# First MLP in token tiles of 512, 512, 512 and 768, the last one's gate and value as seven block products; weight sums over DRAM; q kv in float32

## The chip, the cores and the metric

One NeuronCore of a Trainium2 chip runs the whole program. The metric is the device time of one execution in microseconds (us). The engines are TensorE (PE for the matrix products, PEld for loading their stationary operand), VectorE (DVE), ScalarE (ACT), GpSimd (POOL) and SyncE (SP). SP only issues DMAs; POOL issues DMAs here and little else.

## The reference

Linear attention without a softmax, then two MLPs, all on float32 arrays:

```python
kv  = einsum('bhsd,bhse->bhde', k, v)            # batch 4, 8 heads, 576 tokens, head size 64
out = einsum('bhsd,bhde->bhse', q, kv)
x   = out / sqrt(mean(out*out, -1) + 1e-6) * g_norm   # as 2304 tokens x 512
y   = (1 / (1 + exp(-(x @ w_gate)))) * (x @ w_val) @ w_out    # 512 -> 1536 -> 512
h   = y @ w_in2                                        # 512 -> 2048
res = (maximum(h, 0) + log1p(exp(-abs(h)))) @ w_out2   # 2048 -> 512
```

## The kernel before

Nearly all products are made in three passes: an operand is split into a high part (rounded by ScalarE, `split_hi` L65) and a low remainder (`split_lo` L68, VectorE), and `mm3` (L60) adds high times high, high times low and low times high in PSUM. The instructions of each engine stand in the order in which the code is written (a manual schedule); nothing reorders them, and engines wait for each other by semaphores.

The **first MLP** runs over five token tiles (`TILES1`, L25) of 512, 512, 384, 384 and 512 tokens, and in each over the 12 blocks of 128 hidden columns. I call one block of one tile a unit; there are 60, numbered 0 to 59. A unit is 12 matmuls for the gate (`ffn1_mm`, PSUM tile `ps_g`), 12 for the value (`ps_v`), and 12 that bring the previous unit's gated product back to 512 columns (`ffn1_out` L517, tiles `yacc`), each of as many columns as the tile has tokens. ScalarE takes the sigmoid of the gate, VectorE multiplies it by the value (`gated` L506), and both split the result into the tile `ghl`.

The attention of tiles 2 to 4 is woven into the units of the tile before. It goes in pieces of at most 256 tokens: a transpose of q on VectorE and its split (`q_trans` L434), three passes with the block-diagonal kv of two heads (`po_mm` L441, tile `po`), the square and its split (`po_evac`), two matmuls with a 128x128 matrix that averages over a head (`ss_mm` L457, tile `ss`), a copy of `ss`, a root on ScalarE, and a reciprocal and scaling of 128 partitions on VectorE (`rms_scale` L477).

The **second MLP** runs over three tiles of 768 tokens and eight pairs of hidden blocks each. Its first product is made of 2x2 blocks with seven products in place of eight (`product` L674, PSUM tiles `ps_b` and `ps_c`); the sums of weight blocks that it needs are made beside the first MLP (`m_sums`), stored to DRAM by POOL's queue and loaded again by SP's. The work beside the units is placed by hand: `at_place` (L928) hangs a step on a place of a unit ("A", "B", "C" for matmuls, "a", "bg", "b", "end", "c", "late" for the others), `M_PLAN` (L1016) holds the places of the second MLP's weights, and the main loop (L1128) runs a unit and what hangs on it. The first pair of the second MLP is woven into units 57 to 59.

## Time and profile before

| | |
|---|---|
| time, median of 3 runs | 892.74 us (892.72 to 893.12) |
| the profiled execution's own time | 894.41 us |
| span of its profile | 892.6 us |
| PE, PEld, DVE, ACT busy | 880.7, 780.0, 604.4, 487.4 us |
| DMA traffic | 188.50 MB, 211 GB/s over the span |

Busy time of PE is a union of overlapping records: a matmul of 512 columns is recorded with some 390 ns, but the next one starts some 227 ns after it. So what a run of matmuls takes is read from the start of one group of a timeline to the start of the next, divided by the count, and not from the recorded durations.

### The profile page before, as it was taken

How to read it: one execution, taken by the hardware profiler on the slowest of the kernel's cores; microseconds unless marked ns; L12 is line 12 of the kernel's file. 1: busy time of each engine (PE TensorE's matmuls, PEld its weight loads, DVE VectorE, ACT ScalarE, POOL GpSimd, SP SyncE). 2: the span in 40 equal slices, each digit the busy share in tenths (PEclk: the TensorE clock that was granted, in tenths of full speed). 3: DMA queues.
4: the chain of work that ended last, by engine and by line, in shares of the span. 5: the costliest groups of instructions: out<-in, count | busy, mean ns of one | idle time of the engine just before them, and what ended most of it. 6: DMA issues, size and time to landing. Idle time of an engine off the chain costs nothing.

```text
span 892.6 us, 12252 instructions
## 1 busy us (share of the span) xinstructions
PE 880.7 (99%) x4701; PEld 780.0 (87%) x4701; DVE 604.4 (68%) x884; ACT 487.4 (55%) x778; POOL 72.9 (8%) x112
## 2 busy tenths in 40 slices
PE   7899999999999999999999999999999999999998
PEld 6687888888899999999888889899898989989896
DVE  4888775475856676675577266578776678766666
ACT  5778754544554454643544264556655456554554
...
PEclk9999999999999999999999999999999999999999
...
GB/s 301 283 349 269 190 163 186 283 203 184 236 189 172 99 291 207 175 165 133 303 308 332 141 221 236 203 174 142 236 249 233 225 206 174 140 306 189 188 95 71
DMA packets 89114, 188.50 MB, mean 211 GB/s; under 512 B 35936, under 2 KB 61792, under 8 KB 76768
## 3 DMA queue, kind: packets, MB, share of 16 engines
...
## 4 chain that ended last, share of the span: by engine, by line
PE 95%; DMA 2%; SPq 2%; issue 0%; DVE 0%; ACT 0%
PE oacc L62 22%; PE yacc L62 17%; PE ps_g L62 16%; PE ps_v L62 16%; PE ps_b L680 11%; PE ps_c L680 9%; DMA kv_raw<-in_v_dram 2%; SPq L117 1%; PE kv_ps L272 1%; PE po L62 1%; DMA kv_raw<-in_k_dram 1%; PE o_rows L346 1%; PE qt L334 0%; PE ss L462 0%; PE ss L461 0%; SPq L772 0%
## 5 line engine op out<-in xcount | busy, mean ns | idle before, releaser
L62 PE MATMUL oacc<-w_up,g 128*128 128x512 f32 x864 | 205.2, 391 | 0.0
L62 PEld LDWEIGHTS oacc<-w_up,g 128*128 128x128 f32 x864 | 161.5, 188 | 31.8
L62 PE MATMUL ps_g<-x,w 128*128 128x512 f32 (+1 forms) x720 | 161.2, 372 | 1.5 <-ACT x L396 0.9
L62 PE MATMUL ps_v<-x,w 128*128 128x512 f32 (+1 forms) x720 | 159.8, 370 | 1.3 <-ACT w L66 1.3
L62 PE MATMUL yacc<-ghl,w 128*128 128x512 f32 (+1 forms) x720 | 160.0, 370 | 0.0
L62 PEld LDWEIGHTS ps_g<-x,w 128*128 128x128 f32 x720 | 131.7, 189 | 19.7 <-DVE x L397 1.4
L62 PEld LDWEIGHTS ps_v<-x,w 128*128 128x128 f32 x720 | 129.6, 188 | 18.4 <-ACT w L66 1.7
L62 PEld LDWEIGHTS yacc<-ghl,w 128*128 128x128 f32 x720 | 129.8, 188 | 16.9 <-DVE w L69 0.4
L680 PE MATMUL ps_b<-y_c,w_in 128*128 128x384 f32 x576 | 116.2, 336 | 0.0
L680 PEld LDWEIGHTS ps_b<-y_c,w_in 128*128 128x128 f32 x576 | 102.0, 188 | 2.4 <-DVE y_c L69 0.3
L66 ACT CAST ghl<-sg 128x512 fp32r<-128x512 f32 (+1 forms) x60 | 34.6, 577 | 106.9 <-DVE sg L509 106.9
L680 PE MATMUL ps_c<-y_c,w_in 128*128 128x384 f32 x432 | 87.6, 337 | 0.0
L1078 DVE TENSOR_TENSOR c<-ps_c,c 128x384 f32<-128x384 f32 x72 | 40.1, 557 | 61.1 <-ACT c L1075 31.5
L1075 ACT COPY c<-ps_b 128x384 f32<-128x384 f32 x72 | 34.6, 480 | 81.7 <-PE ps_b L680 80.0
L680 PEld LDWEIGHTS ps_c<-y_c,w_in 128*128 128x128 f32 x432 | 77.0, 188 | 2.1
L503 ACT ACTIVATE sg<-ps_g 128x512 f32<-128x512 f32 (+1 forms) x60 | 33.3, 555 | 74.2 <-PE ps_g L62 72.3
L509 DVE TENSOR_TENSOR sg<-sg,ps_v 128x512 f32<-128x512 f32 (+1 forms) x60 | 37.9, 631 | 51.8 <-PE ps_v L62 50.3
L692 ACT ACTIVATE e<-c 128x768 f32<-128x768 f32 x46 | 39.0, 848 | 49.9 <-DVE c L1078 49.1
L66 ACT CAST g<-c 128x768 fp32r<-128x768 f32 (+1 forms) x50 | 40.6, 812 | 30.9 <-DVE c L717 28.2
L712 DVE SCALAR_TENSOR_TENSOR u<-u,ln 128x768 f32<-128x768 f32 x46 | 43.9, 954 | 12.1 <-ACT ln L704 12.1
L69 DVE TENSOR_TENSOR ghl<-sg,ghl 128x512 fp32r<-128x512 f32 (+1 forms) x60 | 38.1, 635 | 16.8 <-ACT ghl L66 16.5
L69 DVE TENSOR_TENSOR g<-c,g 128x768 fp32r<-128x768 f32 (+1 forms) x50 | 46.2, 923 | 4.5 <-ACT g L66 4.4
...
## 6 DMA issues: line engine op xcount, KB each, us to landing
w_in<-wi_dram SPq DMA_DIRECT2D x42, 1024.0 KB, 6.9
w<-wo_dram SPq DMA_DIRECT2D x24, 1024.0 KB, 5.8
w_up<-wu_dram SPq DMA_DIRECT2D x24, 1024.0 KB, 6.4
...
```

Of the source, the lines that this page charges most:

```text
L62: nc.tensor.matmul(out=ps, lhsT=lhs(a), rhs=rhs(b), start=start and n == 0, stop=stop and n == 2)
L66: nc.scalar.copy(out=hi, in_=src)
L69: nc.vector.tensor_tensor(out=lo, in0=src, in1=hi.bitcast(F32), op=ALU.subtract)
L117: nc.sync.dma_start(out=t, in_=unit(w, f))
L272: nc.tensor.matmul(out=ps[sl, sl], lhsT=lhs, rhs=rhs, start=r == 0, stop=r == R)
L503: nc.scalar.activation(out=sg, in_=chain.pop(("g", t, i)), func=ACTF.Sigmoid)
L509: nc.vector.tensor_tensor(out=sg, in0=sg, in1=chain.pop(("v", t, i)), op=ALU.mult)
L680: nc.tensor.matmul(out=ps, lhsT=w[:, a, kk * P:(kk + 1) * P], rhs=y[:, b, kk], start=first and kk == 0 and n == 0, stop=kk == 1 and n == 2 ...
L692: nc.scalar.activation(out=e, in_=h_t[p][:, f], func=ACTF.Abs)
L712: nc.vector.scalar_tensor_tensor(out=u, in0=u, scalar=1.0, in1=ln_t.pop((p, f)), op0=ALU.subtract, op1=ALU.subtract)
L1075: nc.scalar.copy(out=p_part(n), in_=p_t["b"])
L1078: nc.vector.tensor_tensor(out=h_t[p][:, f, HT * th:HT * (th + 1)], in0=p_t["c"], in1=p_part(n), op=ALU.add)
```

## The change

The first MLP gets four tiles of 512, 512, 512 and 768 tokens, so 48 units in place of 60. The first three run as before. The last one (`unit3`) makes gate and value together as one 2x2 block product: seven products of 6 matmuls of 384 columns (`prod3`) in place of 24 matmuls for each 384 tokens, and 12 matmuls of 512 and 12 of 256 columns for the way back (`out3`). Four of its seven weight operands are sums of blocks of the gate's and value's weights, made on VectorE (`s_whole`, `s_sums`, `s_sums2`), split, stored to DRAM and loaded again (`s_load`), at the places of `S_PLAN`. The seven combinations of x (`x_sub`, `x_comb`) are made before the tile starts. The attention's pieces become 192 tokens (one tile's first piece 128), q times kv is one float32 matmul, the head sums go to 8 rows in place of 128, and their root goes to all partitions over DRAM (`rms_store`, `rms_load`). The second MLP's weights are placed anew; its pair 0 and pair 1 now stand behind the last unit, with the last unit's `out3` between their products.

```diff
-TILES1 = ((0, 512), (512, 512), (1024, 384), (1408, 384), (1792, 512))
+TILES1 = ((0, 512), (512, 512), (1024, 512), (1536, 768))
 TM2, HT = 768, 384
-PIECE = 256
+PIECE = 192
+ORDER = (6, 7, 0, 8, 1, 9, 2, 10, 3, 11, 4, 5)
...
     def po_mm(u, piece, hp):
         b, s0, c0, m = piece
-        ps = atp.tile([P, PIECE], F32, tag="at", name="po")[:, :m]
+        if hp == 0:
+            ss_t[u, c0] = atp.tile([P, 512], F32, tag="at", name="ss")[:8, :m]
+            po_t[u, c0] = atp.tile([P, 512], F32, tag="at", name="po")[:, :m]
+        ps = po_t[u, c0]
         t = hl_t.pop(("q", u, c0, hp))
-        mm3(ps, lambda a: kvb[:, a, hp], lambda b: t[:, b, :m], True, True)
+        nc.tensor.matmul(out=ps, lhsT=kvp[:, (b + 1) % 2, hp], rhs=t, start=True, stop=True)
         at_ps["po", u, c0, hp] = ps
...
     def po_evac(u, piece, hp):
...
         ps = at_ps.pop(("po", u, c0, hp))
         sq = scr.tile([P, PIECE], F32, tag="s", name="sq")[:, :m]
         nc.scalar.activation(out=sq, in_=ps, func=ACTF.Square)
-        nc.vector.tensor_copy(out=of_tile(u)[:, hp, c0:c0 + m], in_=ps)
+        nc.scalar.copy(out=of_rows(u, hp)[:, c0:c0 + m], in_=ps)
         hl_t["s", u, c0, hp] = t = hlpool.tile([P, 2, PIECE], F32R, tag="hl", name="hl")
         split(t[:, HI, :m], t[:, LO, :m], sq)
...
     def ss_mm(u, piece, hp):
         b, s0, c0, m = piece
-        ps = atp.tile([P, PIECE], F32, tag="at", name="ss")[:, :m]
-        t = hl_t.pop(("s", u, c0, hp))
-        nc.tensor.matmul(out=ps, lhsT=ones, rhs=t[:, HI, :m], start=True, stop=False)
-        nc.tensor.matmul(out=ps, lhsT=ones, rhs=t[:, LO, :m], start=False, stop=True)
-        at_ps["ss", u, c0, hp] = ps
-
-    def ss_evac(u, piece, hp):
-        b, s0, c0, m = piece
-        ps = at_ps.pop(("ss", u, c0, hp))
-        if hp == 0:
-            ms_t[u, c0] = stage.tile([P, NP, PIECE], F32, tag="st", name="ms")
-        nc.scalar.copy(out=ms_t[u, c0][:, hp, :m], in_=ps)
+        ps, t = ss_t[u, c0], hl_t.pop(("s", u, c0, hp))
+        for a in (HI, LO):
+            nc.tensor.matmul(out=ps, lhsT=ones[:, hp], rhs=t[:, a, :m], start=hp == 0 and a == HI,
+                             stop=hp == NP - 1 and a == LO, skip_group_check=True)
 
     def rms_root(u, piece):
         b, s0, c0, m = piece
-        ms = ms_t[u, c0][:, :, :m]
-        nc.scalar.activation(out=ms, in_=ms, func=ACTF.Sqrt, bias=eps)
-
-    def rms_scale(u, piece, hps):
+        r = rpool.tile([8, PIECE], F32, tag="r", name="r")[:, :m]
+        nc.scalar.activation(out=r, in_=ss_t[u, c0], func=ACTF.Sqrt, bias=eps[:8])
+        r_t[u, c0] = r
+
+    def rms_store(u, piece):
         b, s0, c0, m = piece
-        ms = ms_t[u, c0][:, hps, :m]
-        of = of_t[u][:, hps, c0:c0 + m]
-        nc.vector.reciprocal(out=ms, in_=ms)
+        nc.vector.reciprocal(out=r_t[u, c0], in_=r_t[u, c0])
+        t0 = TILES1[u][0] + c0
+        nc.sync.dma_start(out=r_dram[:, t0:t0 + m], in_=r_t.pop((u, c0)))
+
...
+    def s_whole(f):
+        s_f[f] = t = block("c1", [P, 8, 256], F32, "s_f")
+        w = W["gv", f]
+        nc.vector.tensor_tensor(out=t[:, :4].rearrange("p (j c) m -> p j (c m)", j=2), in0=w[:, :, HI].bitcast(F32),
+                                in1=w[:, :, LO].bitcast(F32), op=ALU.add)
...
+    def s_sums2(f):
+        w11, w12, w21, w22, s2, s1, s3, s4 = (s_f[f][:, n] for n in range(8))
+        nc.vector.tensor_tensor(out=s2, in0=s1, in1=w11, op=ALU.subtract)
+        nc.vector.tensor_tensor(out=s4, in0=w12, in1=s2, op=ALU.subtract)
+
+    def s_round(f):
+        y = block("c2", [P, 8, 256], F32R, "s_y")
+        s_y[f] = y[:, :4], y[:, 4:]
+        split_hi(s_y[f][HI], s_f[f][:, 4:])
+        if f != ORDER[0]:
+            nc.gpsimd.dma_start(out=ws_dram[f][:, :, HI], in_=s_y[f][HI].bitcast(F32))
+
...
+    def prod3(f, ps, name, comb, first):
+        lhs, x = lhs3(f, name), x_c[comb]
+        for k in range(2):
+            for n, (a, b) in enumerate(PASSES):
+                nc.tensor.matmul(out=ps, lhsT=lhs(a, k), rhs=x[:, b, k],
+                                 start=first and k == 0 and n == 0, stop=k == 1 and n == 2, skip_group_check=True)
+
+    yacc3 = []
...
+        for h in range(2):
+            for m in ms:
+                for n, (a, b) in enumerate(PASSES):
+                    nc.tensor.matmul(out=yacc3[m][h], lhsT=w[:, a, m * P:(m + 1) * P],
+                                     rhs=g[:, b, 512 * h:512 + 256 * h], start=i == 0 and n == 0 and (h == 0 or m % 2 == 0),
+                                     stop=i == F1 - 1 and n == 2, skip_group_check=True)
...
+    def unit3(i, run):
+        f = ORDER[i]
+        pb, pc = (mm.tile([P, TM1], F32, tag="mm", name="ps_" + n)[:, :HT] for n in "gv")
+        p0, p1, p2_, t0, t1, t2 = left
+        add = lambda out, part: nc.vector.tensor_tensor(out=out, in0=pc, in1=part, op=ALU.add)
+        copy, act, mult = nc.scalar.copy, nc.scalar.activation, ALU.mult
+        gap_a, gap_b = gap3(i)
+        prod3(f, pb, "11", "11", True)
+        copy(out=p0, in_=pb)
+        prod3(f, pc, "12", "21", True)
+        add(t0, p0)
+        run("a")
+        prod3(f, pb, "S2", "T2", False)
+        copy(out=p1, in_=pb)
+        act(out=t0, in_=t0, func=ACTF.Sigmoid)
+        run("bg")
+        prod3(f, pc, "S1", "T1", True)
+        prod3(f, pb, "S3", "T3", False)
+        copy(out=p2_, in_=pb)
+        add(t2, p2_)
+        gap_a()
+        run("b")
+        prod3(f, pc, "S4", "22", False)
+        add(t1, p1)
+        prod3(f, pb, "22", "T4", False)
+        act(out=t1, in_=t1, func=ACTF.Sigmoid)
+        g = gl[i]
+        for h, t in ((0, t0), (1, t1)):
+            nc.vector.tensor_tensor(out=t, in0=t, in1=t2 if h else pb, op=mult)
+            split_hi(g[:, HI, HT * h:HT * (h + 1)], t)
+        for h, t in ((0, t0), (1, t1)):
+            split_lo(g[:, LO, HT * h:HT * (h + 1)], t, g[:, HI, HT * h:HT * (h + 1)])
+        run("end")
+        if gap_b:
+            gap_b()
+        run("late")
+
+    Y_HOME = ("b8", "b10", "b11", "b0", "b1", "b2", "b3", "b4", "b5")
     y_raw, y_c, n_y, n_lo = {}, {}, [0], [0]
...
-    M_PLAN = ((30, 35, 36, 40, 40, 50, 50, 54, 56, 61, 62),
...
+    M_PLAN = ((32, 33, 33, 34, 34, 37, 39, 39, 41, 37, 41, 43, 44, 44, 52, 52),
...
+    S_PLAN = ((0, (60, 60, 61, 62, 62)),
+              (1, (63, 65, 65, 65, 66)),
+              (2, (68, 68, 68, 70, 70)),
...
+    y_split("T1")
+    p_open()
+    while n_fed[0] < 5:
+        feed_next()
...
+    s_u(0, 0)
+    s_max(0, 0)
+    out3(last, (1,))
+    p_close()
+    p_start(1)
+    p_11(1)
+    p_copy(0)
+    s_ln(0, 0)
+    s_exp(0, 1)
+    p_12(1)
+    p_add(1, 0, 0, 0)
+    s_u2(0, 0)
+    s_sub(0, 0)
+    s_u(0, 1)
+    y_out3(0)
+    p_s2(1)
+    p_copy(1)
+    s_hi(0, 0)
+    s_max(0, 1)
...
```

How the order of instructions moves, in three places. First TensorE, two units of the 384-token tile 3 before (`po` and `ss` are the attention of the next tile):

```order
L62 MATMUL ps_v<-x,w 128x384 x12
L62 MATMUL po<-hl,kvb 128x256 x3
L62 MATMUL yacc<-ghl,w 128x384 x12
L62 MATMUL ps_g<-x,w 128x384 x12
L461 MATMUL ss<-hl,ones 128x256
L462 MATMUL ss<-hl,ones 128x256
L62 MATMUL ps_v<-x,w 128x384 x12
L62 MATMUL po<-hl,kvb 128x256 x3
L62 MATMUL yacc<-ghl,w 128x384 x12
```

and one unit of the last tile after (`ps_g` and `ps_v` are the two banks of the block products, `x_c` the combinations of x, `s_in` weight sums and `w` or `w_k` weights from DRAM, `yacc` the way back of the unit before):

```order
L668 MATMUL ps_g<-x_c,w_k 128x384 x6
L668 MATMUL ps_v<-x_c,w_k 128x384 x6
L668 MATMUL ps_g<-x_c,s_in 128x384 x6
L668 MATMUL ps_v<-x_c,s_in 128x384 x6
L668 MATMUL ps_g<-x_c,s_in 128x384 x6
L683 MATMUL yacc<-ghl,w 128x512 x6
L683 MATMUL yacc<-ghl,w 128x256 x6
L668 MATMUL ps_v<-x_c,s_in 128x384 x6
L668 MATMUL ps_g<-x_c,w_k 128x384 x6
L683 MATMUL yacc<-ghl,w 128x512 x6
L683 MATMUL yacc<-ghl,w 128x256 x6
```

Three groups of 12 matmuls a unit have become seven of 6 with two groups of 12 between and behind them. Second VectorE, from the last `sg` of one tile into the next; before, from tile 3 into tile 4 (`sg` the gated product, `ghl` its low part, `ys` the copy of `yacc`, `m_raw` and `m_f` second-MLP weights):

```order
L509 TENSOR_TENSOR sg<-sg,ps_v 128x384
L69 TENSOR_TENSOR ghl<-sg,ghl 128x384
L509 TENSOR_TENSOR sg<-sg,ps_v 128x512
L69 TENSOR_TENSOR ghl<-sg,ghl 128x512
L538 COPY ys<-yacc 128x384 x2
L610 SCALAR_TENSOR_TENSOR m_raw<-m_raw 128x1024
L613 SCALAR_TENSOR_TENSOR m_f<-m_raw 128x1024
L509 TENSOR_TENSOR sg<-sg,ps_v 128x512
```

and after, from tile 2 into the last tile (`s_y` the low part of weight sums, `x_c` that of x combinations, `t` the sums and the gated product of `unit3`):

```order
L545 TENSOR_TENSOR sg<-sg,ps_v 128x512
L70 TENSOR_TENSOR s_y<-s_f,s_y 128x1024
L70 TENSOR_TENSOR x_c<-of,x_c 128x768
L70 TENSOR_TENSOR ghl<-sg,ghl 128x512
L70 TENSOR_TENSOR x_c<-of,x_c 128x768 x2
L702 TENSOR_TENSOR t<-ps_v,t 128x384 x2
L576 COPY ys<-yacc 128x512 x2
L798 SCALAR_TENSOR_TENSOR m_raw<-m_raw 128x1024
L702 TENSOR_TENSOR t<-ps_v,t 128x384
L726 TENSOR_TENSOR t<-t,ps_g 128x384
L726 TENSOR_TENSOR t<-t 128x384
L70 TENSOR_TENSOR ghl<-t,ghl 128x384 x2
```

The unit's own additions out of PSUM (`t<-ps_v`) now stand behind the low parts of three combinations of x, of a weight sum and of `ghl`, and one of them behind `ys` and `m_raw`. Third ScalarE in the pair that follows the first MLP; before, from the end of pair 0 into pair 1 (`c<-ps_b` copies a partial sum out of PSUM, `g` is a high part, `e` and `ln` are the softplus of pair 0):

```order
L1081 COPY c<-ps_b 128x384
L692 ACTIVATE e<-c 128x768
L696 ACTIVATE e<-e 128x768
L66 CAST g_4755<-c 128x768
L1075 COPY c<-ps_b 128x384
L704 ACTIVATE ln<-u 128x768
L536 COPY ys<-yacc 128x512
L1075 COPY c<-ps_b 128x384
L536 COPY ys<-yacc 128x512
L1075 COPY c<-ps_b 128x384
```

and after, at the same place:

```order
L890 ACTIVATE e<-e 128x768
L1309 COPY c<-ps_b 128x384
L886 ACTIVATE e<-c 128x768
L1303 COPY c<-ps_b 128x384
L898 ACTIVATE ln<-u 128x768
L890 ACTIVATE e<-e 128x768
L689 COPY ys<-yacc 128x512
L1303 COPY c<-ps_b 128x384
L67 CAST g_4652<-c 128x768
L898 ACTIVATE ln<-u 128x768
L1303 COPY c<-ps_b 128x384
```

The first `c<-ps_b` in either is pair 0's last. Between it and pair 1's first copy stood `abs`, `exp` and `g`, and now `abs` alone; between pair 1's first and second copy stood `ln` and one `ys` copy, and now `ln`, `exp` and `ys`; its third copy now stands behind `g` and `ln` of pair 0.

## Rows read from the trace of the kernel before

**Rows 1.** Page, part 1: busy us (share of the span) xinstructions of the engines.

```profile
PE 880.7 (99%) x4701; PEld 780.0 (87%) x4701; DVE 604.4 (68%) x884; ACT 487.4 (55%) x778; POOL 72.9 (8%) x112
```

**Rows 2.** Page, part 2: busy tenths in 40 slices, and the granted clock.

```profile
PE   7899999999999999999999999999999999999998
DVE  4888775475856676675577266578776678766666
PEclk9999999999999999999999999999999999999999
```

**Rows 3.** Waits of PE: line, releaser: us in total, times, longest; first and last of six.

```profile
PE kv_ps L272 <- DMA kv_raw<-in_v_dram: 2.6, 3, 1.8
...
PE kv_ps L272 <- DMA kv_raw<-in_k_dram: 0.4, 1, 0.4
```

**Rows 4.** Timeline, PE, 384-token tile: start us, us, engine line op out<-in xcount.

```profile
386.16 0.52 PE L62 MATMUL po<-hl,kvb 128*128 128x256 f32 x3
386.51 2.27 PE L62 MATMUL yacc<-ghl,w 128*128 128x384 f32 x12
388.62 2.24 PE L62 MATMUL ps_g<-x,w 128*128 128x384 f32 x12
390.70 0.28 PE L461 MATMUL ss<-hl,ones 128*128 128x256 f32 x1
390.82 0.28 PE L462 MATMUL ss<-hl,ones 128*128 128x256 f32 x1
390.94 2.25 PE L62 MATMUL ps_v<-x,w 128*128 128x384 f32 x12
```

**Rows 5.** Timeline, PE, a 512-token tile.

```profile
235.64 2.88 PE L62 MATMUL yacc<-ghl,w 128*128 128x512 f32 x12
238.36 2.88 PE L62 MATMUL ps_g<-x,w 128*128 128x512 f32 x12
```

**Rows 6.** Timeline, PE, float32 matmuls of 128 columns (two records each).

```profile
57.81 1.05 PE L334 MATMUL qt<-kvf,kv_raw 128*128 128x128 f32 x8
58.62 2.98 PE L62 MATMUL ps_v<-x,w 128*128 128x512 f32 x12
```

**Rows 7.** Timeline, PE, matmuls of 64 columns.

```profile
304.47 0.75 PE L62 MATMUL po<-hl,kvb 128*128 128x64 f32 x6
305.06 2.33 PE L62 MATMUL yacc<-ghl,w 128*128 128x384 f32 x12
```

**Rows 8.** Timeline, PE, block products of the second MLP.

```profile
601.52 1.20 PE L680 MATMUL ps_b<-y_c,w_in 128*128 128x384 f32 x6
602.57 1.23 PE L680 MATMUL ps_c<-y_c,w_in 128*128 128x384 f32 x6
```

**Rows 9.** Lines by form, DVE: names, shapes xcount | busy us, mean ns | idle before.

```profile
L509 DVE TENSOR_TENSOR sg<-sg,ps_v 128x512 f32<-128x512 f32 x36 | 24.6, 684 | 41.7 <-PE ps_v L62 40.4 <-ACT m_raw L129 1.0
L1078 DVE TENSOR_TENSOR c<-ps_c,c 128x384 f32<-128x384 f32 x72 | 40.1, 557 | 61.1 <-ACT c L1075 31.5 <-PE ps_c L680 28.9 <-issue 0.4
L613 DVE SCALAR_TENSOR_TENSOR m_f<-m_raw 128x1024 uint32<-128x1024 uint32 x16 | 19.6, 1226 | 2.5 <-DMA wi_dram<-m_f 2.0
L623 DVE TENSOR_TENSOR m_f<-m_f 128x256 f32<-128x256 f32 x8 | 3.4, 425 | 0.3
L481 DVE RECIPROCAL ms<-ms 128x256 f32<-128x256 f32 x12 | 20.9, 1746 | 0.0
```

**Rows 10.** Lines by form, ACT.

```profile
L704 ACT ACTIVATE ln<-u 128x768 f32<-128x768 f32 x46 | 38.7, 841 | 0.1
L1075 ACT COPY c<-ps_b 128x384 f32<-128x384 f32 x72 | 34.6, 480 | 81.7 <-PE ps_b L680 80.0 <-issue 1.7
L503 ACT ACT_TABLE_LOAD x8 | 10.3, 1283 | 1.2 <-PE ps_g L62 1.1
L536 ACT COPY ys<-yacc 128x512 f32<-128x512 f32 x6 | 3.3, 582 | 0.0
```

**Rows 11.** DMA issues: names, queue, xcount, KB each, median us to landing.

```profile
w<-wo_dram SPq DMA_DIRECT2D x24, 1024.0 KB, 5.8
```

More of the change, by code (lines that the diff above doesn't have):

```diff
@@ new lines, in prod3, with out3 @@
+    def prod3(f, ps, name, comb, first):
[5 more added lines that the diff above has]
+    yacc3 = []
+    def out3(i, ms):
+        f, g = ORDER[i], gl[i]
+        w = W["o", LAST, f]
+        if i == 0 and not yacc3:
+            full = [acc.tile([P, 512], F32, tag="acc", name="yacc") for _ in range(KD)]
+            half = [atp.tile([P, 2, 256], F32, tag="at", name="yacc") for _ in range(2)]
+            yacc3.extend((full[m], half[m // 2][:, m % 2]) for m in range(KD))
+        for h in range(2):
[4 more added lines that the diff above has]
+                                     stop=i == F1 - 1 and n == 2, skip_group_check=True)
@@ L1129, in attention_moe_moe_kernel @@
         prev = its[n - 1]
+        q_prev = prev[1] * (F1 // 2) + prev[2] // 2
+        if t == LAST:
+            unit3(i, lambda place: run(n, place))
+            if i % 2 == 0 and q_prev + 2 < NT1 * F1 // 2:
+                o_load(q_prev + 2)
+            continue
         done = n_l[0]
@@ L1324, in attention_moe_moe_kernel @@
         p_copy(1)
-        if p == 1:
-            y_out(NT1 - 1, 1)
         p_s1(p)
```

401 lines of the change are left out of this document (291 added, 110 removed), and 14 rows, old and new, of the table M_PLAN.

## The prediction

> **What bounds the kernel now.** I read the page's first two parts, then what TensorE waits for, then its timeline. PE is busy 880.7 of 892.6 us [rows 1], at 9 tenths in all but the first and last slice, at the full clock of 2.4 GHz throughout [rows 2]. It was held by six waits in all, which come to 8.0 us (2.6, 2.1, 1.3, 0.9, 0.7 and 0.4), most of them at the start; the first and the last of them stand in [rows 3]. VectorE runs at 4 to 8 tenths and is waited for almost nowhere. So the path that sets the end is the string of matmuls itself, and a change is worth the matmul time that it takes out, less the waits that it puts between them.
>
> What a matmul costs is read from start to start. Twelve of 384 columns take 388.62 - 386.51 = 2.11 us or 390.70 - 388.62 = 2.08 us [rows 4], that is 0.175 us each. Six of a block product, the shape that the new tile uses, take 602.57 - 601.52 = 1.05 us, again 0.175 us each [rows 8]. Twelve of 512 columns take 2.72 us, 0.227 us each [rows 5]. Three of 256 columns take 0.35 us, 0.117 us each, and the two `ss` matmuls of 256 columns 0.12 us each [rows 4]. Six of 64 columns still take 0.59 us, 0.098 us each [rows 7]: I take this for the floor of any matmul with 128 weight columns. The slope from 256 to 512 columns is 0.43 ns a column, one column a cycle, and some 10 ns are added.
>
> **The change part by part.** *The MLP's matmuls.* Out go the two 384-token tiles: 2 x 12 x 36 = 864 matmuls at 0.175 us, 151.2 us. In come 12 units of 42 block-product matmuls (504 x 0.175 = 88.2 us), 12 of 512 columns (144 x 0.227 = 32.7 us) and 12 of 256 columns (144 x 0.117 = 16.8 us), 137.7 us. The other three tiles keep their 512 columns. The gain is 13.5 us. Open is whether 256 columns run at 0.117 us in sixes with a weight load before each, since the trace has them in threes and pairs. The bounds are the floor of 0.098 us and the 0.175 us of 384 columns, 2.7 us better or 8.4 us worse; I take 0.117, which is the same shape.
>
> *The attention's matmuls.* Before, `po` is 36 matmuls of 256 columns at 0.117 us and 48 of 64 to 160 columns between 0.098 and 0.117, say 0.105: 9.3 us; `ss` is 24 at 0.12 and 32 at 0.105: 6.2 us. Together 15.5 us. After, `po` is 28 float32 matmuls. The trace has float32 matmuls of 128 columns as two records each: four take 58.62 - 57.81 = 0.81 us, 0.20 us each [rows 6]. Scaled by columns, 24 of 192 take 0.30 us and 4 of 128 take 0.20, 8.0 us; the lower bound is two floors each, 5.5 us. I take 8.0. `ss` is 56 matmuls with a stationary operand of 8 columns, which the trace does not have: at the floor 5.5 us, at the 0.085 us that 192 columns are by the 512-column row 4.8 us, at 0.12 us 6.7 us. I take 5.5. The gain is 15.5 - 13.5 = 2.0 us, between 0.8 and 5.2.
>
> The four passes that the Trainium skill gives for true float32 ("FP8 and Floating Point Precision", section TensorE Precision Notes) speak against this edit, since the three passes that it replaces become four. By that rule 192 columns cost 4 x 192 / 2.4 = 320 ns, an estimate, and `po` 8.5 us in place of my 8.0; [rows 6] has 0.20 us where the rule has 0.213, so the trace agrees within 5%. The skill's "TensorE: Matmul & The Clock Gate", section LDWEIGHTS, makes a weight load as long as its columns divided by 1.2, in ns. By that an 8-column load vanishes and `ss` goes by its moving columns, 56 x 0.083 = 4.6 us, an estimate; no row here shows such a load.
>
> *What lies beside.* The weight sums cost VectorE, per block, two instructions of 1024 elements (1.23 us) and four of 256 (0.42 us) [rows 9], 4.1 us, 49.7 us for 12, in units 15 to 35, so 2.4 us in a unit of 36 x 0.227 = 8.2 us plus some 0.8 us of attention. VectorE gives back 12 reciprocals of 1.75 us [rows 9] and more for the shorter pieces, and the q splits. At 68% of the span before, it comes to some 85% there: covered, as long as it is never late by more than 5.4 us, since a gate or value bank is used again only after the other's 12 matmuls and `yacc`'s, 2 x 2.72 us. The added DMA (sums and weights stored once and loaded once) goes a unit or two ahead: a 1 MB load lands in 5.8 us [rows 11] and a unit of the last tile is 42 x 0.175 + 12 x 0.227 + 12 x 0.117 = 11.5 us. Inside a unit each bank's copy (0.48 us) [rows 10] or addition (0.56 us) [rows 9] has the next product's 1.05 us to hide in, as in the second MLP's pairs, where the same chain makes PE wait nowhere.
>
> *The waits that it adds*, in three places. First, the entry into the last tile. After the last `ps_v` VectorE has `sg` (0.68), the sum's low part (1.23), three low parts of 768 elements (0.95 each, between 0.56 and 1.23 by [rows 9]), `ghl` (0.69) and the first `t` (0.56): 6.0 us. PE has `yacc` and three products, 2.72 + 3.15 = 5.9 us, before it overwrites the bank, and ScalarE's first copy stands behind its own high parts: 0.5 us. Then the additions stand behind two `ys` copies (0.68 each) and `m_raw` (1.23) after the last `yacc`, so the unit's last addition and multiplication (0.56 each) end some 3.0 us after it, and PE wants the bank after two products, 2.1 us: 0.9 us. Together 1.4 us. Second, two units (seven and eight of the tile) have two low parts or sums of 0.95 to 1.23 us ahead of their first addition, 0.4 us late each: 0.8 us. Third, pairs 0 and 1, which nothing is woven into any more. After pair 0's third product ScalarE makes a copy, a high part (0.84, as the `ln` of as many elements), the table switch (1.28), a copy and another high part, and VectorE its low part [rows 9, 10]: 0.2 + 0.48 + 0.84 + 1.28 + 0.48 + 0.84 + 0.95 = 5.1 us; PE has three products and the `yacc` of one row block (1.03 us), 4.2 us, before it needs that part: 0.9 us. Then pair 0's last copy waits behind `abs` and `exp` (2 x 0.84), and pair 1's first product for the bank: 0.5 us. Pair 1's second copy stands behind `ln`, `exp` and `ys` (2 x 0.84 + 0.58): 0.4 us. Together 1.8 us. Before, none of these places has a wait. The sum of the three is 4.0 us; the lower bound is nothing, if engines run ahead of this order, the upper I put at twice, 8.0 us.
>
> *The sum.* 13.5 + 2.0 - 4.0 = 11.5 us. The profiled span of 892.6 us becomes 881.1, that execution's 894.41 us 882.9. The runs' median is 1.67 us under that execution, so the predicted median is 892.74 - 11.5 = 881.2 us.
>
> **The rivals.** *No wait is added.* The three places hide in slack that I did not see: 892.74 - 15.5 = 877.2 us. For it speaks that an engine ahead of its order costs nothing, against it that the order puts these instructions in front of the ones that PE needs.
>
> *VectorE falls behind in tiles 1 and 2.* If its 85% bunches up so that each of the 21 units with weight sums loses 0.4 us, 8.4 us go: 889.6 us. For it speaks that the units with a reciprocal, two pieces of attention and a second-MLP step sum to some 9.5 us in a unit of 9.0; against it the 5.4 us of slack and lighter units beside them.
>
> *Narrow matmuls.* If the 256-column ones cost 0.175 us, the time is 889.6 us too. The threes at 0.117 us speak against it.
>
> *Slower.* The last tile has two PSUM banks for seven products a unit. If a bank's release comes late at each, with the first addition waiting for the copy of the other bank, PE stands 84 times. The gain is gone from 0.14 us each; at 0.25 us, a quarter of a product, it costs 21 us and the time is 881.2 + 21 = 902 us. For it speaks that VectorE's addition idles for ScalarE's copy 31.5 us in 72 additions in the second MLP [rows 9]; against it that PE does not wait there with the same two banks, at 1.05 us a product.
>
> **How the numbers follow.** Two runs of this kernel are told apart from about 0.2%, 1.8 us: faster is under 890.9, slower over 894.5. I give the forecast, with waits of 2 to 7 us, 0.62 (878.5 to 884.5); no wait 0.16; VectorE behind 0.08; narrow matmuls 0.04; a slower one 0.06; and 0.04 to something that just eats the gain. Faster has 0.62 + 0.16 + 0.07 + 0.03 = 0.88, the same 0.06, slower 0.06. The likeliest is 881.2 us. The range goes from 876.0 (no wait, and a better `ss`) to 888.0 us, which leaves out slower, the same and most of the two cases at 889.6.
>
> **What would show it.** Right: in the last tile a product's six matmuls start 1.05 us apart and six of 256 columns take 0.70 us; the tile's 12 units take 12 x 11.5 = 138 us; PE's waits list names VectorE's additions or `ghl` at the entry, and ScalarE's copies in pairs 0 and 1, with about 4 us. Wrong: waits of PE in units 15 to 35 for `sg`, or any load of `s_in` or `w_k` that PE waits for, or 256 columns at 0.15 us or more. A time over 888 would mean that one of the covers named here does not hold.

## The result, and the profile after

| | us, median (lowest to highest) | ratio to before |
|---|---|---|
| before, in the runs beside it | 892.93 (892.72 to 894.1) | |
| after | 905.25 (903.56 to 908.46) | 1.014 [1.011, 1.0169] |

The kernel became 12.3 us slower; 11.5 us of gain were predicted, so 24 us are to be explained. The profiled execution took 908.46 us with a span of 906.7.

The page, the lines that answer to [rows 1] and [rows 2], and the DMA's share by slices:

```profile
PE 877.4 (97%) x4601; PEld 759.2 (84%) x4601; DVE 621.9 (69%) x915; ACT 504.5 (56%) x797; POOL 98.2 (11%) x147
...
PE   8999999889899988999999999999999999999998
...
DVE  4896876656668648765676476668775688766666
...
PEclk9999999999899999999999999999999999999999
DMA  9996597989978866499897629553556553484521
```

PE is busy for less time than before, as it should be, but it has eights between 159 and 363 us (slices of 22.7 us), and the granted clock its only eight, at 227 to 249 us. VectorE stands at 4 to 8 there, as elsewhere. The DMA stands at 8 and 9 from 159 to 249 us.

What PE waits for (line, releaser: us in total, times, longest), the answer to [rows 3]:

```profile
PE po L473 <- DVE qT L463: 7.6, 5, 2.8
PE ps_v L63 <- DVE sg L545: 3.0, 2, 2.3
PE kv_ps L288 <- ACT r L495: 2.3, 1, 2.3
PE po L473 <- ACT sg L539: 1.8, 1, 1.8
```

Nearly all of this lies in tiles 1 and 2. From 383 us to the end PE's waits come to 0.8 us. Unit by unit (from a unit's first `ps_g` to the next unit's) the loss stands where the waits are. Tiles 0 and 1 took 246.0 us, where they had taken 225.4 with one batch's k and v and 128 tokens' attention less in them, some 5 us. Unit 24, undisturbed, takes 8.8 us; unit 17, with the same work, 13.0; unit 21 16.7, of which 11.4 are matmuls at the full clock; units 29 and 31 12.6 and 12.4, of which 9.3 are. The last tile's 12 units took 138.3 us, 138 predicted.

Part of the loss is the clock. After PE had waited 2.32 us for `sg` in unit 17 and 2.34 us for the root in unit 21, the granted clock stands at 0.50, that is 1.2 GHz, from 197.3 to 200.6 and from 241.7 to 248.3 us. In the second stretch twelve `yacc` matmuls take 248.66 - 243.37 = 5.29 us, for 2.80 in an undisturbed unit:

```profile
241.90 1.53 PE L288 MATMUL kv_ps<-kv_raw 128*64 128x64 f32 x20 [2.34 <-ACT r L495]
243.37 5.36 PE L63 MATMUL yacc<-ghl,w 128*128 128x512 f32 x12
248.66 0.95 PE L288 MATMUL kv_ps<-kv_raw 128*64 128x64 f32 x20
```

With unit 17's `ps_v` (4.06 us for 2.72) the two stretches cost some 4 us, an estimate from these differences. Not every such wait ends so: in unit 15 PE waits 2.85 us for `qT`, and the clock stays at 1.00. The profiles of e2 and e9 have no such stretch in tiles 1 and 2, so that what these runs give back may hold these 4 us too.

Windows (busy us per engine, granted clock, DMA share, GB/s), before and then after, of about the same units:

```profile
165.00:204.00 39.00, 39.00 (x240) 31.46 (x239) 23.80 (x45) 20.36 (x39) 8.91 (x14) 1.00 0.75 234
204.00:246.00 42.00, 42.00 (x192) 34.88 (x191) 30.26 (x40) 20.50 (x31) 9.46 (x14) 1.00 0.60 202
```

```profile
165.00:205.00 40.00, 34.83 (x153) 27.53 (x152) 24.79 (x44) 20.14 (x35) 16.86 (x24) 0.96 0.88 286
205.00:250.00 45.00, 40.76 (x216) 31.69 (x215) 30.28 (x47) 24.62 (x41) 14.59 (x22) 0.92 0.96 303
250.00:300.00 50.00, 49.35 (x240) 40.09 (x239) 37.23 (x64) 25.16 (x48) 13.27 (x19) 1.00 0.82 266
```

VectorE is busy 24.8 of 40 and 30.3 of 45 us, 62 and 67%, where I had put 85%. It was not overloaded, it stood. Its waits and ScalarE's for DMAs are new: in the kernel before, these two engines waited for a DMA once between 130 and 400 us, for 0.2 us.

```profile
DVE of L517 <- DMA ms<-r_dram: 29.2, 6, 8.5
```

```profile
ACT s_y L67 <- DMA wu_dram<-m_f: 5.2, 1, 5.2
ACT m_y L67 <- DMA wu_dram<-m_f: 4.1, 1, 4.1
...
ACT s_y L67 <- DMA ws_dram<-s_y: 3.1, 1, 3.1
```

`ms` is the root of the head sums, broadcast from DRAM. SyncE's queue (its timeline) shows how it comes to be late:

```profile
282.41 10.81 SPq L456 DMA_DIRECT2D q_raw<-in_q_dram  x16
299.99 0.28 SPq L502 DMA_DIRECT2D r_dram<-r  x1
300.33 9.69 SPq L456 DMA_DIRECT2D q_raw<-in_q_dram  x16
310.07 1.25 SPq L509 DMA_DIRECT2D ms<-r_dram  x2
...
325.02 9.98 SPq L456 DMA_DIRECT2D q_raw<-in_q_dram  x16
335.05 1.24 SPq L509 DMA_DIRECT2D ms<-r_dram  x2
```

The answer to [rows 11] is 7.3 us for the same load, and the stores of sums take 5.6 us in the median. In tile 2, which these lines show, the queue stands up to 12.9 us at the root's store until VectorE's reciprocal is done, then spends 10 us on the 16 small DMAs of the next piece of q, and only then sends the broadcast, whose landing VectorE awaits ahead of everything else in its order (2.5, 8.4 and 4.3 us). In tile 1 no q stands between: the broadcasts leave 2.8 to 4.5 us after their store, but the first lands only 9.4 to 11.8 us after its issue, with the DMA's share at 1.0 meanwhile, and VectorE waits 8.5, 4.2 and 1.2 us.

The matmuls' sizes, against [rows 5] and [rows 8]: first an undisturbed 512-token unit, then a unit of the last tile.

```profile
119.21 2.96 PE L63 MATMUL yacc<-ghl,w 128*128 128x512 f32 x12
122.01 2.90 PE L63 MATMUL ps_g<-x,w 128*128 128x512 f32 x12
...
457.96 2.28 PE L683 MATMUL yacc<-ghl,w 128*128 128x512 f32 x12
460.08 1.21 PE L668 MATMUL ps_v<-x_c,s_in 128*128 128x384 f32 x6
461.13 1.20 PE L668 MATMUL ps_g<-x_c,w_k 128*128 128x384 f32 x6
```

A product takes 1.05 us, as predicted. Six `yacc` matmuls of 512 and six of 256 columns take 2.12 us; with 0.227 us for the wide ones the narrow take 0.127, 0.117 predicted (e6 below takes a part of this away). But twelve `yacc` matmuls of a 512-token tile, which the change leaves alone, take 2.80 us where [rows 5] has 2.72.

### The profile page after: what moved, and what is told of

Read it like the earlier page. It is cut to its first block, busy times and chain, and to the rows that moved or that the text cites. A ratio compares the mean times of both kernels' runs of the same rounds, so it can differ in the third digit from the quotient of the medians.

```text
span 906.7 us, 12251 instructions
## 1 busy us (share of the span) xinstructions
PE 877.4 (97%) x4601; PEld 759.2 (84%) x4601; DVE 621.9 (69%) x915; ACT 504.5 (56%) x797; POOL 98.2 (11%) x147
## 5 line engine op out<-in xcount | busy, mean ns | idle before, releaser
L63 PE MATMUL yacc<-ghl,w 128*128 128x512 f32 x432 | 111.6, 407 | 0.0
L63 PE MATMUL ps_v<-x,w 128*128 128x512 f32 x432 | 107.0, 397 | 4.3 <-DVE sg L545 3.0
L63 PE MATMUL ps_g<-x,w 128*128 128x512 f32 x432 | 108.2, 398 | 1.5 <-ACT x L412 0.9
L63 PEld LDWEIGHTS ps_v<-x,w 128*128 128x128 f32 x432 | 80.7, 189 | 22.7 <-DVE sg L545 3.9
L63 PEld LDWEIGHTS ps_g<-x,w 128*128 128x128 f32 x432 | 79.6, 188 | 18.7 <-DVE x L413 1.4
L67 ACT CAST ghl<-sg 128x512 fp32r<-128x512 f32 x36 | 22.4, 621 | 72.5 <-DVE sg L545 72.5
L683 PE MATMUL yacc<-ghl,w 128*128 128x512 f32 (+1 forms) x288 | 54.8, 338 | 0.0
L894 DVE TENSOR_SCALAR u<-e 128x768 f32<-128x768 f32 x46 | 25.6, 557 | 33.5 <-ACT e L890 33.4
```

What stands on the lines that cost most here:

```text
L63: nc.tensor.matmul(out=ps, lhsT=lhs(a), rhs=rhs(b), start=start and n == 0, stop=stop and n == 2)
L67: nc.scalar.copy(out=hi, in_=src)
L683: nc.tensor.matmul(out=yacc3[m][h], lhsT=w[:, a, m * P:(m + 1) * P], rhs=g[:, b, 512 * h:512 + 256 * h], start=i == 0 and n == 0 and (h == ...
L894: nc.vector.tensor_scalar(out=u, in0=e_t[p, f], scalar1=1.0, scalar2=None, op0=ALU.add)
```

## The experiments

Times are medians; the ratio is to runs of the kernel before on the same chip. Four runs of one kernel lie within 3 to 7 us of each other, so that 1 or 2 us between two medians say little. "T01" is the profiled time of tiles 0 and 1 (units 0 to 23), "T2" of tile 2. The profiled execution is one of the runs and can lie some us from their median (the changed kernel's 3.2 and e14's 4.2 us above it, e9's 3.3 and e20's 3.1 us under it), so what T01 and T2 differ by is not what the medians differ by.

| run | us | ratio [95%] | T01 | T2 |
|---|---|---|---|---|
| after | 905.25 | 1.014 [1.011, 1.0169] | 246.0 | 116.6 |
| e1_root_early | 921.45 | 1.0316 [1.0292, 1.034] | 248.1 | 124.7 |
| e2_no_stores | 898.1 | 1.0057 [1.0037, 1.0077] | 233.8 | 116.4 |
| e3_both | 900.02 | 1.0086 [1.0066, 1.0106] | 234.5 | 118.7 |
| e4_kstore_late | 909.85 | 1.0186 [1.0162, 1.0209] | 233.8 | 128.1 |
| e5_kstore_early | 909.84 | 1.0184 [1.0148, 1.0221] | 246.1 | 119.3 |
| e6_pad | 902.46 | 1.0089 [1.0058, 1.0119] | 239.9 | 116.9 |
| e7_no_sums | 896.72 | 1.0035 [1.0024, 1.0046] | 231.6 | 116.2 |
| e8_combo | 907.18 | 1.0155 [1.0133, 1.0177] | 244.6 | 118.9 |
| e9_q_early | 899.52 | 1.0076 [1.0054, 1.0098] | 236.6 | 113.2 |
| e10_q_early_no_stores | 892.59 | 0.9999 [0.999, 1.0008] | 235.8 | 110.4 |
| e11_kstore_sp | 899.64 | 1.0076 [1.0055, 1.0097] | 236.3 | 116.4 |
| e12_all | 893.51 | 1.0012 [0.9991, 1.0032] | 234.7 | 111.9 |
| e13_trans_early | 894.4 | 1.0013 [1.0004, 1.0023] | 238.7 | 110.9 |
| e14_trans_plan | 900.37 | 1.009 [1.0071, 1.011] | 237.0 | 122.7 |
| e17_two_blocks | 891.23 | 0.9975 [0.9964, 0.9986] | 235.3 | 111.5 |
| e18_two_blocks_alone | 904.93 | 1.013 [1.0116, 1.0144] | 241.3 | 117.6 |
| e20_root_first | 891.28 | 0.9978 [0.9965, 0.9991] | 233.0 | 110.3 |
| e21_root_first2 | 888.87 | 0.9946 [0.9931, 0.996] | 231.8 | 112.2 |

**The round trip or the stores.** e1, at `rms_load`:

```diff
-                              in_=r_dram[:, t0:t0 + m]...
+                              in_=wo_dram[0]...[:8, t0 % 1024:t0 % 1024 + m]...
-            at_place(jr + d, c, call(f, u, p))
+            at_place(jr, c, call(f, u, p))
```

> The broadcast of the root (`ms`) is read from 8 rows of stored weights in place of the root's own rows, and issued one unit earlier; the root, its reciprocal and its store stay, and so does every byte that is moved. The scale is therefore by other numbers. Theory A, the round trip over DRAM: VectorE's scale waits 29.2 us in six waits for `ms` in the changed kernel, everything behind it in its order comes late, and TensorE's clock falls after its waits; without the round trip most of the 20.6 us that tiles 0 and 1 lost come back, and a few of tile 2's: 885 to 892 us, and no wait of over 1 us for `ms`. Theory B, the added DMA itself (wk and ws stores) makes loads and the stores whose buffers ScalarE rewrites late: the scale's wait is only where VectorE happened to stand, it stands behind q_raw, m_f or s_y next, and the time stays at 900 to 905 us.

e2 leaves out the stores:

```diff
-        nc.gpsimd.dma_start(out=wk_dram[f]...)   # both
-            nc.gpsimd.dma_start(out=ws_dram[f]...)   # HI and LO
-        nc.sync.dma_start(out=t.bitcast(F32), in_=ws_dram[f])   # and wk_dram[f]
+        nc.sync.dma_start(out=t.bitcast(F32), in_=wo_dram[f // 2]...)
```

> The 6 stores of gate and value blocks (wk) and the 22 of weight sums (ws), 16 MB in all, are left out; the last tile's loads read as many bytes of other stored weights. All sums and casts are still made. The block products are therefore of other numbers. Theory A (round trip): the store and the load of the root still follow each other, at about their least time (3.4 us for the load, 2 to 4 for the store), so VectorE's wait for `ms` shrinks to some 10 us of its 29: 895 to 899 us. Theory B (the DMA's load): the stretches of 165 to 250 us go back to the share of about 0.7 that they had before, q_raw and the casts are on time, and 884 to 890 us follow.

> Both edits: the broadcast of the root from stored rows a unit early, and none of the wk and ws stores. Each theory expects the kernel as I had predicted it, 880 to 886 us. If it stays over 892 us, the loss in tiles 0 and 1 is neither the round trip nor the stores, but the order of the instructions or the narrow products.

The round trip alone falls as the cause: without it the kernel is 16 us slower still, outside both ranges. VectorE's wait for `ms` shrank to one of 5.3 us, and others took its place (waits of ScalarE, then PE, in e1):

```profile
ACT s_y L67 <- DMA ws_dram<-s_y: 20.5, 3, 8.7
...
PE po L473 <- DVE qT L463: 11.8, 3, 7.4
PE po L473 <- ACT of L481: 10.4, 3, 5.7
```

ScalarE rewrites c2, a block of SBUF that the sums share with the second MLP's weights, and must wait until the stores of its last contents have left it. That e3, with the same early broadcasts and no stores, is at 900 us points to the stores as what e1 ran into. The clock takes a part as well: e1's trace has four stretches at a granted 0.50, 23 us in all, where the changed kernel's has two with 10 us. e3 missed the 880 to 886 us that both theories gave it, which by its own rule leaves the order of the instructions or the narrow products. And neither edit took the broadcast from its place on SyncE's queue: in e3 16 DMAs of q still go out from 292.54 to 301.26 us and the broadcast behind them, at 301.78. What they took away is its dependence on the root.

Without the stores alone (e2) 7.2 us come back. That is the range of the first theory (895 to 899 us, and 11.2 us of waits for `ms` where some 10 were expected), not that of the second. By the profile it is all in tile 1, whose DMA share falls to 0.61 and 0.78:

```profile
165.00:205.00 40.00, 37.46 (x173) 30.30 (x173) 30.81 (x50) 23.34 (x40) 8.27 (x12) 1.00 0.61 180
205.00:250.00 45.00, 45.00 (x265) 35.84 (x264) 30.74 (x53) 23.34 (x42) 9.37 (x14) 1.00 0.78 239
```

The first broadcast of tile 1 now lands in 4.7 to 4.9 us in place of 9.4 to 11.8, so one way in which the stores cost is that they slow the round trip. Tile 2 does not gain (one wait for `ms` of 7.9 us stays), and 898 is far from the 881 of the forecast: the stores are a part, and there is another.

**Where the stores are put.** e4, e5 and e11 move the stores of blocks 0 to 5, with one line each:

```diff
-        at_place(12 + f, "late", call(k_store, f))
+        at_place(24 + f, "late", call(k_store, f))        # e4
+        at_place(8 + f // 3, "late", call(k_store, f))    # e5
+        at_place(8, "late", call(k_store, f))             # e11, and nc.sync for nc.gpsimd in k_store
```

> The whole function. The 6 stores of blocks 0 to 5 (4.7 MB) go from units 12 to 17 to units 24 to 29, where DMA is busy 0.6 of the time in place of 0.9. Theory A (round trip): `ms` lands earlier in units 15 to 17 only, 1 to 3 us: 902 to 905 us. Theory B (the DMA's load): a third of the added bytes leave the full stretch of tile 1 and a third of the loss with them: 897 to 900 us.

> The whole function; the same 6 stores of blocks 0 to 5 (4.7 MB), in units 8 and 9 (105 to 122 us, where DMA's share was 0.40). With them in units 24 to 29 the stretch of tiles 0 and 1 had taken 233.8 us, as without any stores, and tile 2 some 12 us more. Theory B, narrowed (a store that meets a full DMA holds the buffers c1 and c2, and ScalarE and VectorE stand behind it in their order): both tiles are spared, 246.0 - 233.8 = 12.2 us come back, 893 us. Rival: the stretch of tile 1 is full by its own sums and second-MLP stores, and these few bytes matter only where they are: the stores of units 8 and 9 push the first second-MLP loads back by as much, 900 to 905 us. Third: the times of tiles 1 and 2 depend on which small delay comes first, and anything between 893 and 910 us may come of a move; then tile 2 differs from its 116.6 us although nothing in it was changed.

> The whole function; the 12 stores of blocks 0 to 5 on SyncE's queue in unit 8, behind the last load of the first MLP's weights. The profile shows no DMA at all from 105 to 115 us, and 4.7 MB take some 15 us at 320 GB/s. (On GpSimd's queue, in units 8 and 9, they had gone out at 64 to 69 and 136 to 139 us, as that queue was free or blocked, and not at 105 us.) Theory B with the place put right: tile 1 is spared them, as in the run with the stores in units 24 to 29 (233.8 us for tiles 0 and 1), and tile 2 keeps its 116.6 us: 892 to 895 us. If small delays decide, 900 to 910 us again.

e4 spares tile 1 as much as leaving out all stores (233.8 us), and tile 2 pays 11.5 us for it, so that the time lies above both ranges. There was no room in units 24 to 29: over their stretch of the changed kernel, 267 to 329 us, the DMA's share is 0.80 and not 0.6. Of the 11.5 us a part is the clock again, with four stretches at 0.50 in tile 2. e5 did not do what its line says (GpSimd's timeline):

```profile
64.57 0.73 POOL L589 DMA_DIRECT2D wk_dram<-w  x1
65.17 0.85 POOL L590 DMA_DIRECT2D wk_dram<-w  x1
...
136.23 0.78 POOL L589 DMA_DIRECT2D wk_dram<-w  x1
```

GpSimd had nothing ahead of them in its order, so three blocks went out over 50 us before their place at the end of unit 8, among the last weights' loads, and three behind a load that waited until 129 us. ScalarE got a weight at 85.3 us (80.1 in the changed kernel) and unit 5 took 18.3 us in place of 12.0. In e11 the stores stand in SyncE's order behind the last weight, where the trace of the changed kernel has a gap:

```profile
105.00:110.00 5.00, 5.00 (x26) 4.12 (x25) 4.97 (x5) 4.54 (x6) 0.00 (x0) 1.00 0.00 2
110.00:115.00 5.00, 5.00 (x23) 4.04 (x23) 4.22 (x5) 5.00 (x7) 0.00 (x0) 1.00 0.03 7
```

That gave 5.6 us, half of what I expected, all in tile 1.

**Place in SBUF.** e6:

```diff
+    const.tile([P, 96], F32, name="const_pad")
     g_col = const.tile([P, 1], F32, name="g_col")
```

> The changed kernel with 96 unused floats per partition ahead of `g_col`, so that everything in SBUF that follows the constants lies where it lay before (the head-sum matrix had 512 bytes per partition and has 128 now). The twelve `yacc` matmuls of an undisturbed unit took 2.79 us, 2.72 before, with the gate's and value's unchanged. If it is the place of the weights against that of the gated values in SBUF, a unit takes 8.16 us again instead of 8.25, and 36 units give 3 us: 902 us. If not, 905 us and 8.25 us a unit.

The median fell by 2.8 us, no more than the spread of the runs (898.8 to 903.5 us); what shows the cause is the unit, which takes 8.16 us again. The same unit as above now reads

```profile
120.22 2.88 PE L63 MATMUL yacc<-ghl,w 128*128 128x512 f32 x12
122.94 2.43 PE L63 MATMUL ps_g<-x,w 128*128 128x512 f32 x10
```

2.72 us from start to start. The change made `ones` 384 bytes smaller, and with it the weights moved against `ghl`, which lies at SBUF's other end. The last tile's `yacc` gains too: six matmuls of 512 and six of 256 columns take 2.09 us in place of 2.12.

**VectorE's load.** e7 is e2 with

```diff
-    for f, slots in S_PLAN:
+    for f, slots in S_PLAN[-1:]:
```

> No wk and ws stores, as in the run at 898.1 us, and no weight sums either but those of the first block of the last tile (11 of 12 left out, 45 us of VectorE and 14 of ScalarE's casts); the last tile's loads read other stored weights. If the rest of the loss (898 against the 881 predicted) is VectorE and ScalarE coming late with `qT` and `sg` under the added sums, tile 2 goes from 116.4 to some 108 us and the time to 886 to 889 us. If it is the attention's new order (the transposes of q behind the head sums' low parts, two matmuls in a row for each), the waits of 1.33 us for `qT` in every second unit of tile 2 stay, and 895 to 898 us come out.

45 us less work on VectorE are worth 1.4 us, which these runs hardly tell from nothing; tile 2 stays at 116.2 us, and VectorE still waits 20.0 us for `ms`. With the queue as it was, VectorE's load is not what costs; with the queue mended it was not tried. e8 is e5 and e6 with larger pieces:

```diff
-    ws_dram = dram.tile([F1, P, 4, 2, 256], F32, name="ws_dram")
+    ws_dram = dram.tile([F1, P, 2, 4, 256], F32, name="ws_dram")
```

> The whole function: the stores of blocks 0 to 5 in units 8 and 9, the 96 floats of padding, and the sums' high and low parts stored as pieces of 4 KB in place of 1 KB. If the first two act as hoped, 893 - 3 = 890 us; if pieces of 4 KB also shorten the 22 stores' 5.6 us, one or two us less; if pieces of 1 KB moved as fast, nothing. By the third theory (sensitive to any small delay) the sum of the parts does not hold.

It is 17 us over the 890 hoped for, as the stores went out early again, and 2.7 us better than e5, which e6 alone explains; unit 5 took 19.2 us, much as in e5. The larger pieces gave nothing that shows.

**SyncE's queue.** e9 places five loads of q earlier, e10 does so without the stores.

```diff
+    LOAD_Q = {(2, 0): 10, (2, 1): 11, (2, 2): 15, (3, 0): 22, (3, 1): 23, (3, 2): 25, (3, 3): 27}
-        at_place(j0 - 2, "late", call(load_q, u, p))
+        at_place(LOAD_Q[u, n], "late", call(load_q, u, p))
```

> The whole function. Only the places of five of the seven loads of q change (units 11, 15, 23, 25, 27 in place of 13, 16, 24, 26, 28), so that on SyncE's queue the 16 DMAs of a piece stand ahead of the `ys` stores and no longer between a piece's root store and its broadcast. Theory C (SyncE's queue in its order: it stands at the root's store for the reciprocal, then takes 9 to 19 us over 16 DMAs of q, and the broadcast that VectorE waits for stands behind them): VectorE's wait for `ms` goes from 29.2 us to under 12, that for q_raw to nothing, and 895 to 899 us follow. Theory B (the stores fill the DMA): the order on the queue is worth little, 903 to 906 us.

> The same, without the wk and ws stores (the last tile's loads read other stored weights). Without the stores alone it was 898.1 us, with tile 2 at 116.4 us and VectorE waiting for `ms` 7.9 us at a time. Theory C: tile 2 comes down to 108 to 110 us, the time to 889 to 891 us. If tile 2 stays at 116 us, its waits of TensorE for `qT` come from VectorE's own order, and the time stays at 896 to 898 us.

Both went the way of the theory of the queue, 5.7 us by itself, though each ended just outside its range (899.5 us; 892.6 us, with T2 at 110.4), and the waits for `q_raw` stayed at 4.2 us. In tile 2 the broadcast now follows its store by 2.7 us in place of 10.1 (timeline of e9):

```profile
293.03 0.28 SPq L502 DMA_DIRECT2D r_dram<-r  x1
295.77 1.25 SPq L509 DMA_DIRECT2D ms<-r_dram  x2
297.72 15.65 SPq L456 DMA_DIRECT2D q_raw<-in_q_dram  x16
```

VectorE's wait for `ms` fell from 29.2 to 11.4 us, without stores to 3.3; units 29 and 31 take 10.0 and 9.3 us, 5.7 less. Queue and stores add up: 7.2 and 5.7 by themselves, 12.7 together. By the profile e9 gains in tile 1 as well (T01 236.6 for 246.0), where no q had stood between; the first broadcast there lands in 6.3 to 7.2 us, and no stretch is left at half the clock, but why it lands sooner is not shown.

**Together, and what is left.** e12 is e6, e9 and e11: 893.5 us, 11.7 of their 14.1 us, and in none of the ranges below.

> The whole function: q loaded early, the stores of blocks 0 to 5 on SyncE's queue in unit 8, and the 96 floats of padding (worth 2.8 us by itself). If B and C each hold for a part: 905 - 12 - 7 - 3 = 883 us. If they are one loss told twice: 889 to 892 us. Over 895 us both are wrong as a remedy.

e13 moves transposes, e14 also six steps of `M_PLAN` and these sums:

```diff
-            at_place(j - 1, "late", *[call(q_trans, u, p, h) for h in hh])
+            at_place(j - 1, "bg" if (u, n) in ((2, 1), (2, 2)) and j == j0 else "late", *[call(q_trans, u, p, h) for h in hh])
-              (7, (99, 100, 101, 101, 101)),      (8, (102, 103, 103, 105, 106)),     # e14
+              (7, (100, 101, 102, 102, 103)),     (8, (104, 104, 105, 106, 107)),     # e14
```

> The whole function: the run at 893.5 us (q early, stores of blocks 0 to 5 on SyncE's queue, padding) with the first two transposes of the second and third piece (in units 14 and 17) at the unit's start in VectorE's order in place of its end. In that run unit 15 takes 13.6 us and TensorE waits 2.9 us for `qT`, with VectorE's transposes behind a second-MLP step that waits for its load, its store and ScalarE, and behind the reciprocal. If VectorE's order is what is left, unit 15 takes about 9.3 us and 4 us go: 889 to 890 us. If the step itself (its load and store) is, TensorE waits as long for the next of VectorE's results, `sg`, and the time stays at 893 us.

> The same, and in units 24 to 27 six second-MLP steps and two blocks' weight sums each one place later, so that the transposes of unit 24 do not stand behind both the `ys` copies and the step. There TensorE waits 1.0 us for ScalarE's `of` and 0.8 us for `qT`, and units 24 and 25 take 2.2 us too long in all. If VectorE's order is what is left, another 1 to 2 us go: 887.5 to 889 us. If the delay only moves to units 26 to 28, where the sums now stand closer together, it is the same as without it.

Neither gave anything in time (894.4 and 900.4 us). In e13 unit 15 came down from 13.6 to 10.1 us, but units 19 to 21 gave back 6.3: ScalarE met the stores in c2 again. In e14 the sums stand closer together, and T2 is 11.8 us longer by the profile, the medians by 6.0. In tile 2 of that profile are two stretches of 6.6 us at a granted 0.50, behind waits of PE of 3.35 and 4.77 us, so a part of it is the clock (waits of ScalarE for these blocks in e13, then in e14):

```profile
ACT s_y L67 <- DMA wu_dram<-m_f: 5.3, 1, 5.3
ACT s_y L67 <- DMA ws_dram<-s_y: 4.4, 1, 4.4
```

```profile
ACT s_y L67 <- DMA ws_dram<-s_y: 13.1, 2, 8.3
ACT s_y L67 <- DMA wu_dram<-m_f: 11.7, 2, 6.4
```

e17 gives four blocks' sums another block of SBUF on top of e13, e18 does it alone in the changed kernel.

```diff
-        y = block("c2", [P, 8, 256], F32R, "s_y")
+        y = block("o2" if f in (0, 2, 3, 5) else "c2", [P, 8, 256], F32R, "s_y")
```

> The whole function: the run at 894.4 us (q early, stores on SyncE's queue, padding, transposes early), with the rounded sums of blocks 0, 2, 3 and 5 in block o2, which lies free in tile 1, in place of c2. In that run unit 15 had got 3.5 us shorter and units 19 to 21 5.8 us longer, where ScalarE's `s_y` cast waits 5.3 and 4.4 us for the stores that still read c2. If that single block, handed from sums to second-MLP steps with a store to wait for each time, is what sets tile 1's pace (theory D), these waits go, units 19 to 21 are 9.3, 8.7 and 11.4 us, and 888 to 890 us follow. If it is the DMA's load, the casts wait no longer but something else does (m_raw, `ms`), and it stays at 893 to 895 us.

> The changed kernel, whole function, with that one edit alone (blocks 0, 2, 3 and 5 in o2). Theory D: tile 1 wins several us by it, 897 to 901 us. Theory of the DMA's load: the stores of units 15 to 21 are issued earlier, into a DMA that is already full, and 903 to 906 us come out.

The sums' casts (`s_y`) wait for no store any more in either (in e18 the cast `m_y` still does, for 4.9 us), but alone that is worth nothing, with 25.3 us of waits for `ms` where there were 29.2. On top of the others it is worth 3.2 us, with units 19 to 21 still 4.3 us too long and the time between the two ranges. So c2 is one wait in a ring of them, and theory D fails as the one pace. The last two go after ScalarE's order:

```diff
-              (3, (82, 82, 82, 82, 82)),        (4, (83, 83, 85, 85, 85)),
+              (3, (83, 83, 83, 83, 83)),        (4, (84, 84, 85, 85, 85)),      # e20
-              (46, ..., 53, 56, 56, 57, 57, 58, 58), (58, 65, ...
+              (46, ..., 53, 56, 56, 57, 59, 59, 59), (60, 65, ...               # e21 as well
```

> The whole function: the run at 891.2 us with one block's weight sums (3) one place later in unit 20, and the next (4) with it, so that ScalarE takes the third piece's root ahead of the `s_y` cast. In that run the root stands behind the cast (1.05 us), and the cast behind VectorE's five sums (4.3 us); `kv_ps` waits 1.5 us for the root, which frees its PSUM bank, then 1.3 us for the copy `kvp`, and unit 21 takes 14.3 us instead of 11.4. If the order on ScalarE is what is left there, 2.9 us go: 888 to 889 us. If the wait comes back in units 22 and 23 (sums of block 5, the split of x), 891 us.

> The same, and in unit 14 the first piece's root ahead of the second-MLP step's cast `m_f`, which waits for a store; the load behind that step goes from unit 14 to 15. In the run at 891.2 us unit 15 takes 10.6 us where units 18 and 19 without a wait take 8.7 and 9.3. If the root's place decides, 1 to 1.5 us more go: 887 to 888 us. If the step is only put off, it comes back in units 16 to 19: the same as without it.

e20 changed nothing in the median, though unit 21 of its profiled execution is 1 us shorter. e21 took unit 15 to 8.8 us and is the fastest version, 0.54% under the kernel before; e17 and e20 are 0.25 and 0.22% under it. What PE still waits for in tiles 1 and 2 of it:

```profile
PE po L474 <- DVE qT L464: 2.6, 3, 1.4
PE kv_ps L289 <- ACT kvp L301: 1.7, 1, 1.7
...
PE po L474 <- ACT of L482: 1.4, 1, 1.4
```

## Why the prediction was wrong

**The step that failed** is the part on what lies beside. Its sentence "the added DMA (sums and weights stored once and loaded once) goes a unit or two ahead" looked at the loads of the last tile alone. They are on time. The stores were never priced. From 205 to 250 us, in tile 1, the DMA's share is 0.96 with them and 0.78 without (e2); a block that is stored can't be rewritten before it has left, and the small broadcast lands late. e2 measures it at 7.2 us.

**A part left out.** "VectorE gives back 12 reciprocals" booked the gain of the 8-row root and not what replaces them: a store, a load that waits for it, and both on a queue on which in tile 2 16 DMAs of q stand between. I had costed no DMA that the moved steps issue, nor read SyncE's order past them. With q ahead of the root 5.7 us came back (e9), while the dependence on the root, taken away with the queue as it was, gave nothing (e1 and e3).

**The cover.** "Covered, as long as it is never late by more than 5.4 us": the condition was right, the reason to think it held was not. 85% busy was too high, and busy share was the wrong measure: VectorE was busy 62 to 67% and late by up to 8.5 us, because it waits in order. The prediction's own sign of being wrong came: PE waits 3.0 us for `sg`, beside 7.6 for `qT`, which it had not named. Nothing in it allows for the clock, which fell behind two of the waits and cost some 4 us more. The rival that had VectorE behind named the place, at 8.4 us and a chance of 0.08, but the load (e7, 1.4 us) is not what held it.

**The matmul sum** was right in the large: the last tile 138.3 us for 138. Of its sizes, 256 columns took 0.127 us for 0.117 (1.4 us); with e6's padding they take 0.121, so over half of this is the place in SBUF and not the shape. From e2's units 18 (two `po`, 8.80 us) and 20 (four `ss`, 8.75) against 8.25 without: `po` takes 0.275 us of the unit's time, 7.7 us in all for 8.0, and `ss` 0.125, 7.0 us for 5.5. The four passes of the Trainium skill ("FP8 and Floating Point Precision", TensorE Precision Notes) gave an estimate of 0.32 us for such a `po`; the measured 0.275 is 14% less. The Trainium skill's "TensorE: Matmul & The Clock Gate", section LDWEIGHTS, by which a load of 8 columns vanishes, gave an estimate of 4.6 us for `ss`; the measured 7.0 us do not agree, and whether it is the load that takes the rest is not shown. The 2.8 us that `yacc` lost by its place in SBUF (e6) were in no term.

**The added waits**, 4.0 us, were too many: in the last tile PE waits 0.3 us where I had 2.2, and pairs 0 and 1 take 20.3 us against 18.8 of matmuls, 1.5 us for my 1.8. Two readings on the way were wrong, with little weight for the time: the addition and multiplication behind `ys` and `m_raw` at the entry come to 3.7 us by the terms given, not 3.0; and the clock was not full throughout, as the kernel before has 3.3 us at a granted 0.50 from 42.6 us, which a digit of 9 does not show. The slower rival, two banks late at 84 products, did not happen.

**What the 24 us are.** Stores and queue 12.7 us (e10), SBUF's place 2.8 (e6), orders on VectorE and ScalarE with a second block for the sums 4.6 (893.5 to 888.9, e13 to e21): 20.1, on different bases, so that the sum is a rough one. Of the rest, some 6 us stand in e21's units 21, 24, 25 and 28 as waits for `kvp`, `qT` and `of`, which no run took away. By what PE does in the profiled execution, its waits come to 24.9 us where 12.0 were forecast (8.0 before and 4.0 added), and the clock adds some 4. Open is also why e1 lost as much as 16 us: beside the clock, that it is the ring of waits over c2 is argued from e3, e13 and e14, and no run with e1's edit and a second block was made.
